# Loading each token-pair tile by four transfers of one head in place of one transfer of four heads

## The chip, the cores, the metric

One core of a Trainium2 chip. The metric is the device time of one launch in microseconds (us). Run-to-run spread is about 1 us for the kernel before. Times within a trace count from the start of its span, which is about 1.7 us shorter than the device time. "Granted clock" is the share of its full clock that TensorE was given; PSUM is the memory into which this kernel's matmuls write.

## The reference

```python
def _attn_ref(q, k, v):                       # q, k, v: (8, 8, 576, 64) float32
    scores = (1/sqrt(64)) * q @ k^T
    Dmat = where(rel >= 0, gamma[h] ** rel, 0)    # rel = query position - key position
    return (scores * Dmat) @ v

def reference(q, k, v, w_gate, w_val, w_out):
    x = attn_out.transpose(0, 2, 1, 3).reshape(4608, 512)
    return (sigmoid(x @ w_gate) * (x @ w_val)) @ w_out     # d_ff = 1536
```

## The kernel before

Everything is loaded by one instruction queue, SP (SyncE), in program order. First come the tokens of two "pairs" (a pair is 256 tokens, two neighbouring tokens on one partition), then the FFN weights, then a third pair between the rows of the output weights (wo), then the per-step loads of the rest.

```python
ld_pool = ctx.enter_context(tc.tile_pool(name="ld", bufs=18))
PAIRS = [(0, 0), (0, 1), (1, 0)]

def load_pair(A):
    b, a2 = PAIRS[A]
    for nm, src, g in (("k", k, 0), ("q", q, 0), ("k", k, 1), ("q", q, 1), ("v", v, 0), ("v", v, 1)):
        t = ld_pool.tile([P, M, 2, D], FP32, tag="ld", name=f"{nm}32p_{A}_{g}")   # M = 4 heads, 256 KB
        nc.sync.dma_start(out=..., in_=...)          # the change is here
        parts[nm, "pair", A, g] = t
        yield

for A in range(2):
    for _ in load_pair(A):
        pass
load_w(0, 2); load_w(2, 2); load_w(4, 4); load_w(8, 4)      # 24 tiles of 256 KB
pair_2 = load_pair(2)
for n_wo, n_pair in ((2, 4), (6, 2), (4, 0)):               # 2 wo, k q k q, 6 wo, v v, 4 wo
    ...
```

Each tile is cast as a whole, then transposed, multiplied and so on. This is what POOL and ACT do around the third pair:

```python
# ... cut: FFN of the first 512 tokens, whose matmuls run on TensorE between these lines
turn("k", 2, 0, tr_psum, "tr")     # turn: transpose on TensorE, copy out of PSUM on ACT
cast_wo(3, on_act)
turn("q", 2, 0, pv_psum, "pv")
cast_wo(4, on_pool)
turn("k", 2, 1, tr_psum, "tr")
turn("q", 2, 1, pv_psum, "pv")
# ... cut
cast_pair("v", 2, 1, on_pool)
cast_wo(9, on_pool); cast_wo(11, on_pool)      # wo 8 and 10 on ACT
loads_to(1)                                    # v, k, q of steps 0 and 1
# ... cut
later_constants()                              # mask tri, on POOL
for t in vbd[2:4]:
    nc.gpsimd.memset(t, 0.0)
casts_to(1)                                    # k, q of step 0 on POOL, then DMA transpose T, then v
```

T is a DMA transpose of step 0's k and q; the first per-step matmul (qk) needs it.

## Time and profile before

| | before |
|---|---|
| device time, median of 3 runs | 336.96 us |
| TensorE busy | 328.0 us of a span of 335.4 |
| first FFN matmul, hg | 19.60 us |
| first weight issued by SP / last wo tile landed | 9.90 us / 46.20 us |
| T landed / first qk that reads it | 57.11 us / 57.61 us |

The table of windows for the kernel before cuts the span at hg, at the landing of the last wo tile, and at the first qk. Its columns are the stretch and its length, then the busy time of each engine (with counts), TensorE's granted clock, the share of the DMA engines and GB/s:

```profile
0.00:19.60 19.60, 16.12 (x249) 8.49 (x249) 12.52 (x38) 11.90 (x24) 11.48 (x24) 1.00 0.99 275
19.60:46.20 26.60, 26.60 (x177) 12.55 (x178) 16.62 (x26) 14.20 (x26) 16.07 (x24) 1.00 1.08 349
46.20:57.60 11.40, 11.05 (x121) 6.06 (x119) 4.45 (x8) 4.85 (x11) 10.37 (x19) 1.00 0.74 149
57.60:335.40 277.80, 274.27 (x2242) 157.17 (x2240) 130.57 (x259) 136.84 (x285) 147.25 (x262) 1.00 0.81 157
```

TensorE is full from hg on, and the DMA engines are full until the last wo tile. The landing time of T is its issue at 53.33 us plus the 3.8 us that the tile view gives.

### The profile page before, as it was taken

What the parts mean: (1) busy time and instruction counts of PE and PEld (TensorE: products, weight loads), DVE (VectorE), ACT (ScalarE), POOL (GpSimd) and SP (SyncE); (2) the same over time, 40 slices, a digit from 0 to 9 for tenths busy, and PEclk for the clock granted to TensorE, in tenths of its full rate; (3) what the DMA queues carried; (4) which work ended last, traced back from release to release, by engine and by line L of the source; (5) the groups of instructions that cost most, each with busy time, mean ns of one, the idle gap of its engine ahead of it and who ended that gap; (6) DMA issues with size and microseconds to landing.
All of it is one profiled execution on the core that took longest, in us unless ns stands there. A gap on an engine that the chain in (4) does not pass through costs nothing.

```text
span 335.4 us, 7396 instructions
## 1 busy us (share of the span) xinstructions
PE 328.0 (98%) x2784; PEld 184.3 (55%) x2784; DVE 164.2 (49%) x328; ACT 167.8 (50%) x345; POOL 185.2 (55%) x327
## 2 busy tenths in 40 slices
PE   7999999999999999999999999999999999999996
PEld 3544445969666566556566555445555455444443
DVE  5744755726376356436346635542574156503320
ACT  6545635637565456355456655445646455233321
POOL 5655679779868798882448966582577500000000
PEclk9999999999999999999999999999999999999999
DMA  7999996799999999999976999499773850020002
GB/s 210 313 372 359 335 255 131 139 225 201 174 214 193 186 205 211 214 247 214 225 132 125 185 240 199 106 232 247 136 135 82 254 203 2 0 95 33 0 31 96
DMA packets 164100, 60.00 MB, mean 179 GB/s; under 512 B 144480, under 2 KB 156000, under 8 KB 164064
## 3 DMA queue, kind: packets, MB, share of 16 engines
q1 hardware_dynamic: 163920, 59.39, 83.2%
q8 instruction: 22, 0.36, 0.5%
q10 hardware_dynamic: 144, 0.13, 0.1%
q14 instruction: 14, 0.11, 0.1%
HBM read 37.75 MB, written 9.44 MB: 141 GB/s over the span
## 4 chain that ended last, share of the span: by engine, by line
PE 94%; DMA 2%; DVE 1%; SPq 1%; issue 1%; ACT 0%; POOL 0%
PE h L495 49%; PE op L561 24%; PE op L745 3%; PE hg L610 3%; PE hv L610 3%; PE pv L420 2%; PE qk L399 2%; PE pv L418 2%; DMA k32p<-in_k_dram 2%; PE st L432 2%; SPq L114 1%; PE op L551 1%; PE pvp L370 1%; PE idle L159 1%; PE st L345 0%
## 5 line engine op out<-in xcount | busy, mean ns | idle before, releaser
L495 PE MATMUL h<-xT,wg_sb 128*128 128x384 bf16 (+2 forms) x480 | 102.8, 337 | 0.2 <-DVE gv L523 0.2
L495 PE MATMUL h<-xT,wv_sb 128*128 128x384 bf16 (+2 forms) x480 | 102.8, 337 | 0.0
L252 POOL TENSOR_TENSOR qk_nat<-k,ktab 64x256 bf16<-64x256 f32 x120 | 73.3, 611 | 42.9 <-PE st L432 27.5
L523 DVE TENSOR_TENSOR gv<-g,h 128x384 bf16<-128x384 bf16 (+1 forms) x96 | 59.6, 621 | 71.8 <-PE h L495 56.4
L561 PE MATMUL op<-wo_sb,gv 128*128 128x512 bf16 x372 | 85.5, 379 | 0.0
L519 ACT ACTIVATE g<-h 128x384 bf16<-128x384 f32 (+1 forms) x96 | 52.2, 544 | 64.9 <-PE h L495 58.3
L438 DVE CAST sbd<-st 64x256 bf16<-64x256 f32 x104 | 43.7, 420 | 45.1 <-PE st L432 42.9
L495 PEld LDWEIGHTS <-wg_sb 128*128 128x128 bf16 x480 | 43.7, 98 | 31.4 <-issue 0.4
L495 PEld LDWEIGHTS <-wv_sb 128*128 128x128 bf16 x480 | 44.1, 98 | 29.0 <-issue 0.4
L273 POOL CAST vbd<-v 64x256 bf16<-64x256 f32 x120 | 47.4, 395 | 15.2 <-PE pv L420 10.6
L561 PEld LDWEIGHTS <-gv 128*128 128x128 bf16 x372 | 34.4, 98 | 36.3
L538 ACT COPY ob<-op 128x512 f32<-128x512 f32 x33 | 19.3, 585 | 47.5 <-PE op L561 42.8
L283 ACT CAST vs<-v 64x256 bf16<-64x256 f32 x104 | 41.9, 403 | 1.6
L262 POOL TENSOR_TENSOR qk_nat<-q,qtab 128x512 bf16<-128x512 f32 (+1 forms) x34 | 35.4, 1041 | 2.6
L422 ACT CAST xT<-pv 128x512 bf16<-128x512 f32 (+1 forms) x34 | 18.1, 534 | 18.1 <-PE pv L420 18.0
L401 DVE TENSOR_TENSOR pt<-qk,tri 128x512 bf16<-128x512 f32 (+1 forms) x34 | 21.2, 625 | 6.1 <-PE qk L399 5.8
L420 PE MATMUL pv<-pt,vbd 128*128 128x64 bf16 x240 | 18.0, 193 | 0.0
L432 PEld LDWEIGHTS <-qk_nat 128*128 128x128 bf16 x208 | 13.2, 98 | 8.8
L420 PEld LDWEIGHTS <-vbd 128*128 128x128 bf16 x240 | 15.2, 98 | 3.5
L418 PE MATMUL pv<-T,sbd 128*128 128x64 bf16 x216 | 17.2, 193 | 0.0
L511 DVE TENSOR_TENSOR gv<-g,h 128x256 bf16<-128x256 bf16 x24 | 10.0, 420 | 13.7 <-ACT g L509 13.3
L418 PEld LDWEIGHTS <-sbd 128*128 128x128 bf16 x216 | 15.1, 98 | 2.5
(76 smaller groups left out, 232.8 us busy)
## 6 DMA issues: line engine op xcount, KB each, us to landing
out_dram<-ob SPq DMA_DIRECT2D x34, 256.0 KB, 2.8
v<-in_v_dram SPq DMA_DIRECT2D x26, 256.0 KB, 4.1
k<-in_k_dram SPq DMA_DIRECT2D x26, 256.0 KB, 4.6
q<-in_q_dram SPq DMA_DIRECT2D x26, 256.0 KB, 5.1
wg<-in_moe_w_gate_dram SPq DMA_DIRECT2D x12, 256.0 KB, 6.0
wv<-in_moe_w_val_dram SPq DMA_DIRECT2D x12, 256.0 KB, 5.8
wo<-in_moe_w_out_dram SPq DMA_DIRECT2D x12, 256.0 KB, 5.4
k32p<-in_k_dram SPq DMA_DIRECT2D x6, 256.0 KB, 5.6
```

What stands on the lines that cost most here:

```text
L252: nc.gpsimd.tensor_tensor(out=kn[half(hh), j, :, half(hh)], in0=k32[half(j), hh::2, :], in1=ktab[half(j), c, hh::2].unsqueeze(2).to_broadc ...
L262: nc.gpsimd.tensor_tensor(out=qs[0:n], in0=q32[0:n], in1=qtab[0:n, c, :].unsqueeze(2).to_broadcast([n, H, D]), op=ALU.mult)
L273: nc.gpsimd.tensor_copy(out=vb[half(hh), j, :, half(hh)], in_=v32[half(j), hh::2, :])
L283: nc.scalar.copy(out=natural["vs", s][half(hh), j], in_=loaded[s][0][half(j), hh::2, :])
L401: nc.vector.tensor_tensor(out=pt[:, :, 0:n].rearrange("p m (j t) -> p m j t", t=64), in0=qkp[:, :, 0:n].rearrange("p m (j t) -> p m j t", ...
L418: nc.tensor.matmul(pvp[:, m, half(j)], lhsT=before[:, m, :], rhs=qT[:, m, half(j)], start=True, stop=False)
L420: nc.tensor.matmul(pvp[:, m, half(j)], lhsT=vb[:, j, m, :], rhs=pt[:, m, half(j)], start=before is None, stop=True)
L438: nc.vector.tensor_copy(out=sb[half(hh), :, half(hh)], in_=st_tiles[b][half(hh)])
L495: nc.tensor.matmul(out, lhsT=w_sb[:, kc, fc * P:(fc + 1) * P], rhs=xT[:, kc, t0 + a:t0 + e], start=(kc == 0), stop=(kc == NKC - 1))
L519: nc.scalar.activation(out=g[:, 0:n], in_=h1[:, 0:n], func=AF.Sigmoid)
L523: nc.vector.tensor_tensor(out=gvs[some[0]][:, a:e], in0=g[:, 0:n], in1=h2[:, 0:n], op=ALU.mult)
L561: nc.tensor.matmul(opp, lhsT=gvs[fc][:, nb * P:(nb + 1) * P], rhs=wo_sb[:, fc, :], start=(fc == 0), stop=(fc == NFC - 1))
```

## The change

Intent: an earlier start of the first tiles, as each head's piece can land by itself. Bytes and layout are the same.

```diff
             t = ld_pool.tile([P, M, 2, D], FP32, tag="ld", name=f"{nm}32p_{A}_{g}")
-            nc.sync.dma_start(
-                out=t.rearrange("p h r d -> p h (r d)"),
-                in_=src[b, g * M:(g + 1) * M, a2 * 2 * P:(a2 + 1) * 2 * P, :].rearrange("h (p r) d -> p h (r d)", r=2))
+            for h in range(M):
+                nc.sync.dma_start(
+                    out=t[:, h].rearrange("p r d -> p (r d)"),
+                    in_=src[b, g * M + h, a2 * 2 * P:(a2 + 1) * 2 * P, :].rearrange("(p r) d -> p (r d)", r=2))
```

## The prediction

> **What bounds the kernel now.** I read the page first. TensorE is busy 98% of the span and is 94% of the chain that ended last, so once TensorE is fed, the end lies a fixed amount of matmul work later. The question is therefore when TensorE gets fed. In forty slices (8.4 us each) its row shows the one soft place, the first slice, and the row of the DMA engines shows them full there:
>
> ```profile
> PE   7999999999999999999999999999999999999996
> DMA  7999996799999999999976999499773850020002
> ```
>
> Second, the chain of waits in order of time, restricted to the start. From 4.11 to 10.01 us the chain is a token pair load (the first k tile of the second pair), then a POOL cast, then a densely packed row of small matmuls up to the first FFN matmul (hg) at 19.60 us:
>
> ```profile
> 4.11 5.90 DMA k32p<-in_k_dram
> ...
> 10.08 1.05 POOL kp L242
> ...
> 14.54 1.29 DVE ptp L335 x2
> ...
> 19.60 1.02 PE hg L610 x4
> ```
>
> From hg on nearly every piece is TensorE work, so a later hg moves the end by the same amount. Third, the timeline of the SP queue, which issues every load (start, duration, what). It shows the pieces that the change multiplies, a kind with the shape of the new pieces (weight and output rows: one run per partition), and the issue of the first weights, which stands behind all twelve pair tiles:
>
> ```profile
> 1.32 0.49 SPq L114 DMA_DIRECT2D q32p<-in_q_dram  x1
> 1.85 0.51 SPq L114 DMA_DIRECT2D k32p<-in_k_dram  x1
> 2.40 0.51 SPq L114 DMA_DIRECT2D q32p<-in_q_dram  x1
> ...
> 9.90 1.34 SPq L126 DMA_DIRECT2D wg<-in_moe_w_gate_dram  x2
> ...
> 34.06 1.80 SPq L132 DMA_DIRECT2D wo<-in_moe_w_out_dram  x4
> ...
> 223.85 2.04 SPq L533 DMA_DIRECT2D out_dram<-ob  x4
> ```
>
> Fourth, the consumers. The casts on POOL begin as each tile lands; each has an idle time ended by the DMA:
>
> ```profile
> 3.94 1.04 POOL L242 TENSOR_TENSOR kp<-k32p,ktab 128x512 bf16<-128x512 f32 x1 [1.02 <-DMA k32p<-in_k_dram]
> 6.33 1.04 POOL L242 TENSOR_TENSOR kp<-k32p,ktab 128x512 bf16<-128x512 f32 x1 [1.35 <-DMA k32p<-in_k_dram]
> 10.08 1.04 POOL L242 TENSOR_TENSOR kp<-k32p,ktab 128x512 bf16<-128x512 f32 x1 [0.31 <-DMA k32p<-in_k_dram]
> 11.88 1.04 POOL L242 TENSOR_TENSOR kp<-k32p,ktab 128x512 bf16<-128x512 f32 x1 [0.76 <-DMA k32p<-in_k_dram]
> ```
>
> So in the first 15 us the kernel is bound by the pair loads: 256 KB land every 0.9 us (10.08 to 11.88 is two tiles), near 290 GB/s.
>
> **What the Trainium skill says.** "DMA: Bandwidth & Descriptors", section "Rules for kernel authors", says to coalesce small transfers, and that under 64 KB one pays mostly overhead; the new pieces are exactly 64 KB. "Issuing engines are not separate DMA queues", same page, calls the sequencer's time to start a DMA usually small relative to the DMA. The trace agrees for 256 KB (0.49 to 0.51 us of issue against 0.9 us of transfer); for 64 KB it cannot hold, since an estimated quarter of the transfer, 0.22 us, is less than half an issue. "Perfetto Trace Analysis", "What 'DMA-bound' means", names this state: the issuing sequencer's track is solid DMA slices.
>
> **The change part by part.** Bytes, and runs of 512 B, stay the same. Each pair tile takes 4 issues in place of 1: 18 issues become 72. The built order of SP confirms it (229 rows become 277, with repeats folded) and keeps the order of everything else. The first 12 tiles, 48 issues, still stand ahead of the first weight. The order also shows that the eight completion semaphores are used in rotation, so at most 8 pieces (512 KB) are in flight, where 8 tiles (2 MB) were; and each consumer now waits on four semaphores.
>
> Cost of one issue when they follow each other: the four wo issues took 1.80/4 = 0.45 us, the four stores 2.04/4 = 0.51; the pair issues 0.51 plus 0.04 of gap. The new pieces have one run per partition, like wo and stores, so I take 0.48 us from start to start (estimate). Eight of these are 3.8 us, more than a piece's landing time, so the rotation should not stop them. Landing time: the first 256 KB took 3.0 us (the tile view's minimum); less three quarters of 0.9, about 2.1 to 2.3; I take 2.1.
>
> Tile j (from 0) is then complete at 0.80 + 0.48(4j+3) + 2.1 = 4.3 + 1.92j. The last q tile of the second pair (j = 9), whose cast began at 12.74 before, lands at 21.6: 8.9 us later. The last v tile (j = 11) lands at 25.5, against 14.4. From the q tile on I walk the chain: cast 0.7, transpose and copy to 23.5, qk, the two masks on DVE at 1.29 us a pair (23.0 to 24.3, 24.75 to 26.05), v cast at 26.1, then st, filler matmuls, pv and the copy to xT, 2.3 us more: hg at about 28.4 in place of 19.6. **+8.8 us.** The small matmuls and fillers between wait inside that time and add nothing.
>
> Weights: first issue at 0.80 + 48 x 0.48 = 23.8 in place of 9.90. The first two wg tiles land about 26.7 and 27.5 and are cast by 28.2, just ahead of hg. At the 351 to 384 GB/s that the table of windows gives for 15 to 25 us, 256 KB come every 0.68 to 0.75 us, against 0.86 us of matmul per tile (3.45 us per 16). So the stream holds, with its former 4 us of lead gone: +0 to 1 us.
>
> The third pair, loaded between wo tiles at 29.3 to 38 us: 24 issues in place of 6. The DMA queue is full there, so the first eight pieces only wait for older tiles; the next eight run at 0.48 and leave the DMA engines half idle. My walk has its tiles land 10.1, 10.4, 11.5 and 12.6 us later than before while TensorE is 8.8 later: +1.4 us of stall at their transposes. The following v tiles come 13.4 later against a little slack: +0.7. The first per-step loads (v, k, q after wo) come about 14 us later against 2 us of slack at POOL's casts at 49.53; I give +1.5. Sum: 8.8 + 1.4 + 0.7 + 1.5 = 12.4, so 337 + 12 = **349 us**.
>
> **The rivals.** (1) The loads stay hidden: a quicker issue. A store issued after a pause needs only about 0.33 us, and at 0.37 start to start the same formula gives the q tile 4.3 us less delay: +4.5 at hg, and with half of the rest about 343. For it: smaller transfers generate fewer runs per issue. Against it: the two fours above, which are the back-to-back case. (2) The earlier first piece helps: consumers could start at the first head. The code casts a whole tile and the built order has the cast wait for all four semaphores, so no gain. (3) Eight semaphores in rotation become the wait: if a piece landed in 4.8 us, the pace would be 0.6 us and hg would slip by another 39 x 0.12 = 4.7 us: about 354. Against it: the first landing, 3.0 us for four times the bytes. (4) TensorE's clock: the skill's "TensorE: Matmul & The Clock Gate", "HAM oscillation", says idle gaps above about 3.4 us bring back half rate. The page before shows a granted clock of 9 tenths or more throughout; my walk leaves gaps of 1 to 2 us, so I expect little, at worst 2 us more.
>
> **Range and chances.** 343 is the quick-issue case, 355 the rotation case or the clock case, so **343 to 355** should hold it 8 times in 10. Slower by over 2% means over 343.7: 0.88. Within 2%: 0.11 (quick issue, or the later stalls absorbed). Faster: 0.01, as nothing on the path gets shorter.
>
> **What would show it.** SP's timeline: 48 pieces spaced by 0.45 to 0.5 us and the first wg issue at 23 to 25 us. The share of DMA in the first two slices falls while SP is solid. Fourth k cast near 20 us. First hg near 28.4. Later: a wait of about 1 us before the third pair's transposes, and hg to the end longer by 2 to 4 us than the 315.8 of before. It is wrong if pieces are spaced by 0.37 or less, if their landing takes over 4 us, or if the stages after hg give time back.

## The result

The changed kernel takes 357.34 us (median of 4 runs, 356.8 to 358.44) against 337.41 for the kernel before in the same rounds. The ratio is 1.0594, with a 95% interval of 1.0558 to 1.063. A ratio is the mean time of one kernel's runs over that of the other's of the same rounds, so it is not quite the ratio of the medians. The direction was right; the size was 20 us in place of 12, outside the predicted range. All outputs are right.

The page of the changed kernel, in forty slices of the span (8.9 us each): TensorE, its granted clock, and the DMA engines.

```profile
PE   6679976989999999999999999999999999999996
PEclk9859998999999999999999999999999999999999
DMA  4449958969999999999998599969964790011002
```

TensorE is now soft in six of the first nine slices, not in one. The DMA engines are half idle in the first three and in the sixth. The granted clock falls twice, right where TensorE is thin.

SP's queue in the changed kernel (start, duration, what, count):

```profile
2.67 1.85 SPq L115 DMA_DIRECT2D q32p<-in_q_dram  x4
4.57 1.85 SPq L115 DMA_DIRECT2D k32p<-in_k_dram  x4
...
15.97 3.14 SPq L115 DMA_DIRECT2D k32p<-in_k_dram  x4
...
24.85 0.95 SPq L127 DMA_DIRECT2D wg<-in_moe_w_gate_dram  x2
```

A tile of four pieces starts every 1.90 us, 0.475 us a piece, with no pause in between: SP's track is solid while the DMA engines are about half idle (a share of 0.54 up to hg). One tile is slower, 3.14 us. The weights are issued 15 us later than before.

The table of windows, cut at the same three events:

```profile
0.00:30.58 30.58, 20.28 (x246) 10.33 (x250) 12.24 (x37) 12.15 (x24) 10.44 (x22) 0.78 0.54 148
30.58:67.00 36.42, 30.31 (x217) 13.64 (x221) 17.73 (x26) 14.69 (x27) 17.13 (x26) 0.95 0.85 277
67.00:78.05 11.05, 9.14 (x82) 4.99 (x78) 5.30 (x10) 5.83 (x14) 10.01 (x19) 1.00 0.77 154
78.05:356.10 278.05, 272.85 (x2213) 157.16 (x2240) 129.39 (x255) 135.75 (x282) 148.09 (x262) 1.00 0.82 157
```

Up to hg the loss is 11.0 us. From hg to the last wo landing it is 36.42 - 26.60 = 9.8 us more. The last two rows are as long as before, within 0.4 us. So everything was lost before the last wo tile landed, at 67.00 us in place of 46.20.

TensorE's waits after hg, from its timeline (the bracket is the idle time before, and what ended it):

```profile
49.84 0.40 PE L312 MATMUL kTp<-ident,kp 128*128 128x128 bf16 x4 [1.20 <-POOL kp L243]
...
53.68 0.40 PE L312 MATMUL kTp<-ident,kp 128*128 128x128 bf16 x4 [1.50 <-POOL kp L243]
...
57.97 0.38 PE L312 MATMUL qTp<-ident,qp 128*128 128x128 bf16 x4 [3.03 <-ACT qT L322]
...
78.05 0.41 PE L400 MATMUL qk<-T 128*128 128x64 bf16 x8 [1.40 <-DMA T<-qk_nat]
```

It looks as if the third pair's transposes cost 5.7 us, and ACT the most of it. That reading fell in the experiments. The chain of waits of the changed kernel, followed back from the end, does not go through these transposes; before the first qk it goes through POOL, and before that through the load of a wo tile:

```profile
62.27 4.73 DMA wo<-in_moe_w_out_dram
67.00 0.05 issue
67.06 0.62 POOL wo_sb L225
...
73.08 1.04 POOL qk_nat L263
...
74.15 3.86 DMA T<-qk_nat
78.00 0.05 issue
78.05 0.41 PE qk L400 x8
```

The same place in the kernel before, POOL and TensorE from the timeline:

```profile
46.25 0.61 POOL L224 CAST wo_sb<-wo 128x512 bf16<-128x512 f32 x1 [0.83 <-DMA wo<-in_moe_w_out_dram]
52.26 1.04 POOL L262 TENSOR_TENSOR qk_nat<-q,qtab 128x512 bf16<-128x512 f32 x1
57.61 0.40 PE L399 MATMUL qk<-T 128*128 128x64 bf16 x8
```

POOL takes the same 7 us from the wo cast to T's issue in both kernels (46.25 to 53.33, 67.06 to 74.15). Before, T landed at 57.11 and TensorE came at 57.61 without a wait: it was the later one by half a microsecond.

### The profile page after: what moved, and what is told of

Read it like the earlier page. It is cut to its first block, busy times and chain, and to the rows that moved or that the text cites. A ratio compares the mean times of both kernels' runs of the same rounds, so it can differ in the third digit from the quotient of the medians. Undisturbed runs are those within 1.5% of the kernel's fastest.

```text
span 356.1 us, 7450 instructions
## 1 busy us (share of the span) xinstructions
PE 332.6 (93%) x2749; PEld 186.1 (52%) x2784; DVE 164.7 (46%) x328; ACT 168.4 (47%) x345; POOL 185.7 (52%) x327
## 3 DMA queue, kind: packets, MB, share of 16 engines
q1 hardware_dynamic: 164784, 59.40, 79.4%
## 4 chain that ended last, share of the span: by engine, by line
PE 76%; SPq 9%; DMA 8%; issue 3%; POOL 2%; DVE 1%; ACT 1%; DVEq 0%
PE h L496 45%; PE op L562 22%; SPq L115 7%; DMA wo<-in_moe_w_out_dram 4%; DMA wg<-in_moe_w_gate_dram 3%; PE pv L421 2%; PE qk L400 2%; PE pv L419 2%; PE st L433 2%; SPq L127 1%; DMA T<-qk_nat 1%; PE op L552 1%; POOL qk_nat L253 1%; DVE ptp L336 0%; PE hv L611 0%
## 5 line engine op out<-in xcount | busy, mean ns | idle before, releaser
L562 PE MATMUL op<-wo_sb,gv 128*128 128x512 bf16 x356 | 84.5, 379 | 0.8
L433 PEld LDWEIGHTS <-qk_nat 128*128 128x128 bf16 x208 | 13.2, 98 | 8.8
L419 PE MATMUL pv<-T,sbd 128*128 128x64 bf16 x216 | 17.2, 193 | 0.0
```

Of the source, the lines that this page charges most:

```text
L419: nc.tensor.matmul(pvp[:, m, half(j)], lhsT=before[:, m, :], rhs=qT[:, m, half(j)], start=True, stop=False)
L562: nc.tensor.matmul(opp, lhsT=gvs[fc][:, nb * P:(nb + 1) * P], rhs=wo_sb[:, fc, :], start=(fc == 0), stop=(fc == NFC - 1))
```

## The experiments

Twelve kernels ran. First the table that they give together; each time is from the profiled run of that kernel, and the ratio from all its timed runs. "whole" means unsplit pair tiles.

| kernel | hg | last wo landed | T landed | first qk | span | ratio to before |
|---|---|---|---|---|---|---|
| before | 19.60 | 46.20 | 57.11 | 57.61 | 335.4 | 1 |
| the change | 30.58 | 67.00 | 78.00 | 78.05 | 356.1 | 1.0594 |
| first_two | 30.09 | 59.40 | 70.39 | 70.43 | 347.9 | 1.0376 |
| third | 19.74 | 54.08 | 65.02 | 65.45 | 343.1 | 1.0191 |
| two_halves | 22.51 | 49.97 | 60.87 | 60.91 | 338.6 | 1.0098 |
| empty_issues (whole) | 31.30 | 59.73 | 70.68 | 71.32 | 348.8 | 1.0398 |
| empty_all (whole) | 29.98 | 67.29 | 78.25 | 78.30 | 356.0 | 1.0604 |
| split_wo_late | 32.25 | 66.03 | 76.98 | 77.03 | 355.0 | 1.0589 |
| third_wo_late | 20.27 | 52.47 | 63.38 | 63.43 | 341.1 | 1.0190 |
| whole_wo_late | 20.19 | 46.69 | 57.69 | 58.20 | 336.0 | 1.0003 |
| split_warm | 29.14 | 65.54 | 76.51 | 76.56 | 355.6 | 1.0557 |
| split_T_early | 29.73 | 65.56 | 75.17 | 76.05 | 354.1 | 1.0540 |
| split_both | 30.00 | 65.61 | 74.82 | 74.87 | 352.9 | 1.0519 |
| whole_T_early | 19.60 | 45.81 | 55.09 | 57.62 | 335.4 | 0.9991 |

From the first qk to the end is 277.5 to 278.1 us in every row but split_warm, which has 279.1. The kernels of first_two, split_wo_late, split_T_early and split_both are the changed kernel up to hg, and still hg lies between 29.73 and 32.25 us in these five rows: a difference of 1 or 2 us at hg between two single profiles shows nothing. T lands 10.9 to 11.0 us after the last wo tile in every row but the three in which POOL's order was changed.

### Which loads cost: first_two and third

```diff
-            for h in range(M):                     # four pieces, all pairs
+            if A < 2:                              # first_two;   third: if A == 2
+                for h in range(M): ...             # four pieces
+            else:
+                nc.sync.dma_start(...)             # one transfer
```

> Only the two pairs loaded ahead of the weights are split, the third pair stays whole. Theory (issue time at the start sets hg, the third pair has a cost of its own): hg at 30.6 us as in the changed kernel (30.58), then half or more of the later loss gone: 348.5 to 351. Rival (the later loss is only the lost lead of the weights, not the third pair's own pieces): 355 to 357. Rival (the start costs what I predicted and the rest is the third pair): 346 to 347.

Measured: 349.92 us (349.46 to 350.58), +3.8%; hg at 30.09.

> Only the third pair is split. Theory: hg at 19.6 us as before, then TensorE waits at the third pair's transposes, above all the last q one, whose copy on ACT stands behind the cast of a wo tile that is now issued after 16 pieces: 341 to 344. Rival (the 4 us of lead that the weights still have here hides it): 337 to 339.

Measured: 344.28 us (341.69 to 344.78), +1.9%, a little above the range that I gave; hg at 19.74.

The two parts add up: 3.8% and 1.9% make 5.7% of the 5.9%. In terms of the last wo landing they are +13.2 and +7.9 us, together 21.1 of the measured 20.8. So the third pair's 18 extra issues cost 7.9 us, close to their issue time (18 x 0.475 = 8.6), though the weights had their lead there. But issue time is not the only wait there. SP's waits between 41 and 64 us in the changed kernel, for the pieces of the third pair (total us, times, longest):

```profile
SPq L115 <- DMA wo<-in_moe_w_out_dram: 2.5, 5, 1.1
SPq L115 <- DMA wv<-in_moe_w_val_dram: 1.3, 4, 0.3
SPq L115 <- DMA wg<-in_moe_w_gate_dram: 0.6, 2, 0.3
```

Each of these eleven issues waits for a semaphore that an older tile holds (the one at 59.03 us for the wo tile that landed at 59.01), as eight completion semaphores are used in rotation. SP stood 4.4 us for them in all. At the start no piece waits so. No run gives the third pair more semaphores, so how its 7.9 us divide between issue time and this limit of eight transfers in flight is not shown.

### Half the split: two_halves

```diff
+            for h in range(0, M, 2):
+                nc.sync.dma_start(out=t[:, h:h + 2]..., in_=src[b, g * M + h:g * M + h + 2, ...]...)
```

> Every pair tile in two transfers of two heads. Theory (the issue rate of SP against the landing rate): two issues at about 0.52 us are 1.04 us a tile, little over the 0.9 us at which whole tiles landed, so hg slips by only 0.5 to 1.5 us and the first wg issue moves from 9.9 to about 13.3: 338 to 340. Rival (cost goes by the size of a transfer or by the number of semaphores waited for, so half the split costs about a third to a half): 344 to 348.

Measured: 340.74 us (339.62 to 341.41), +1.0%, between the theory's range and the rival's, and far nearer the theory's. SP needs 0.51 us from start to start (4.37, 4.89, 5.40 us), so 1.03 us a tile against the 0.9 us at which whole tiles landed. hg came 2.9 us late, more than the 0.5 to 1.5 that I expected. A slow stretch is part of it: the transfer issued at 9.49 us landed 2.0 us after the one before it. Cost is not in proportion to the number of pieces. The three points (0.55 us of issue a tile before, 1.03 and 1.90) fit a cost that sets in where the issue time of a tile passes its transfer time.

### Issues alone, tiles whole: empty_issues and empty_all

```diff
             nc.sync.dma_start(out=t..., in_=...)                # whole tile, as before
+            for x in range(3 if A < 2 else 0):                  # empty_all: range(3)
+                nc.sync.dma_start(out=spare[:, at:at + 4], in_=k[0, x, 0:P, 0:4])
+                at += 4
```

> Kernel before with whole tiles, but each of the first twelve pair tiles is followed by three transfers of 16 bytes a partition into a spare tile that nobody reads: the 36 issues of the split without the split. Right results. Theory (SP's issue time): period about 1.95 us a tile, first wg issue near 24 us, hg near 28 to 30.5 us, 347 to 351, as in the run that splits the first two pairs alone. Rival (64 KB transfers, pieces in flight or four semaphores a cast are the cost): 337 to 340.

Measured: 350.82 us (350.0 to 351.38), +4.0%; hg at 31.30, first weight issued at 25.24 us.

> Kernel before with whole tiles, and three empty issues of 16 bytes a partition after every one of the 18 pair tiles, the third pair too. Right results. Theory (the whole loss is issue time in SP's queue, which delays the last wo tile; the end follows that landing, and the two stretches add): last wo tile lands at 66 to 67.5 us, as in the changed kernel (67.00), 355.5 to 358.5. Rival (the third pair's cost is its small pieces or their semaphores): 350 to 352, as with 36 empty issues.

Measured: 357.62 us (357.29 to 359.1), +6.0%; last wo tile landed at 67.29 us (67.00 in the changed kernel). SP's queue in empty_all:

```profile
4.79 0.44 SPq L117 DMA_DIRECT2D k32p<-in_k_dram  x1
5.27 1.45 SPq L121 DMA_DIRECT2D spare<-in_k_dram  x3
6.77 0.43 SPq L117 DMA_DIRECT2D q32p<-in_q_dram  x1
7.25 1.45 SPq L121 DMA_DIRECT2D spare<-in_k_dram  x3
```

An issue of 2 KB that nobody reads takes the same 0.48 us as one of 64 KB. These kernels have the whole tiles of before, one semaphore per cast for each tile, and the whole loss. This settles what costs: neither the split of the tiles nor the number of semaphores that a cast waits for is needed for it. The extra issues are enough. At the start they cost by SP's time alone; in the third pair the empty issues wait in the rotation of eight as the pieces do, so the two stay together there.

### Is it ACT's order? split_wo_late, third_wo_late, whole_wo_late

My second theory was built on the 3.03 us above. ACT stood in front of wo tile 3, which is issued after 16 pieces of the third pair, so ACT could not empty the PSUM buffer that TensorE's last q transpose needed.

```diff
-    cast_wo(3, on_act)
     turn("q", 2, 0, pv_psum, "pv")
 ...
     turn("q", 2, 1, pv_psum, "pv")
+    cast_wo(3, on_act)
```

> The changed kernel, with one ACT instruction moved: the cast of the wo tile number 3 stands after the copy of the third pair's last transpose in place of before the q copy of its first half. Theory (ACT stands in front of a late wo tile and keeps a PSUM buffer that TensorE's last q transpose needs): that transpose comes at about 55.7 us in place of 57.97, the end 2 to 4 us earlier than the changed kernel: 353.5 to 355.5. Rival (the last q tile's own landing at 54.7 us is the whole wait): 356.5 to 358.

Measured: 357.19 us (356.76 to 357.78), +5.9%: no change.

> The same move in the kernel that splits the third pair alone, where TensorE stood 4.66 us for ACT's copy. Theory: 2.1 us of the wait stay (the q tile's landing), 2.5 go, and with the shorter pause the granted clock does not fall to a half: 340 to 342 in place of 344.3. Rival: 343.5 to 345.

Measured: 343.98 us (342.77 to 344.28), +1.9%: no change (third had 1.9% too).

> Control: the same move in the kernel before. Theory (wo tile 3 lands there just in time, so ACT's order costs nothing): 336.5 to 338, same as before. Rival (the move is a gain by itself, whatever the loads): 334 to 336.

Measured: 337.45 us, ratio 1.0003 (0.9988 to 1.0018): no change, as expected.

The theory is half right, and of no use for the time. TensorE's timeline in split_wo_late:

```profile
55.28 0.40 PE L312 MATMUL qTp<-ident,qp 128*128 128x128 bf16 x4 [0.18 <-DVE qp L243]
...
77.03 0.41 PE L400 MATMUL qk<-T 128*128 128x64 bf16 x8 [1.98 <-DMA T<-qk_nat]
```

The wait at the transpose is gone (0.18 in place of 3.03 us), and the wait for T has grown (1.98 in place of 1.40). In third_wo_late the wait, which had been 4.66 us in third, fell to 0.52 the same way. What was taken from TensorE's chain was given back at T, since T hangs on the load stream. In third itself T had landed only 0.4 us before TensorE came (65.02 and 65.45), so no more than that was to be gained.

### Is it the clock? split_warm

```diff
     turn("k", 0, 0)
+    fill(4)                        # filler matmuls, no result
     turn("q", 0, 0)
-    fill(4)
+    fill(9)
 ... cut: seven more places, 35 more fillers in all (the expectation says 37)
```

> The changed kernel with 37 more filler matmuls in front of the transposes at which TensorE stood idle in the first 25 us; the loads are untouched. Theory (about 1 to 1.5 us of the loss up to hg is the granted clock, which fell to 0.5 to 0.77 between 10 and 30 us): clock 1.0 through the start, hg near 29.5 in place of 30.58, 355 to 356.5. Rival (landing times alone set hg, the clock costs nothing there): clock 1.0 and 357 to 358.

Measured: 356.65 us (355.17 to 357.33), ratio 1.0557 (1.0532 to 1.0583), whose interval overlaps that of the changed kernel: not settled. What the profile settles is the clock. In the table of windows for 10 to 30 us, the changed kernel has a mean granted clock of 0.66 and split_warm 1.00:

```profile
10.00:30.00 20.00, 14.49 (x219) 7.98 (x222) 7.74 (x12) 6.90 (x14) 5.77 (x8) 0.66 0.58 161
```

```profile
10.00:30.00 20.00, 16.19 (x244) 8.49 (x238) 8.05 (x13) 7.28 (x15) 5.15 (x7) 1.00 0.57 159
```

hg came at 29.14 us, earlier than in the five profiles that are alike up to there (29.73 to 32.25), but by an amount that one profile can't tell. TensorE then waited 1.80 us for the second weight tile in the middle of hg: the loads were behind it all the same. After that wait the clock fell again (0.66 from 30 to 35 us), so this run does not show the kernel at full clock throughout.

### Is it T? split_T_early, split_both, whole_T_early

The third theory: two chains meet at the first qk, and in the changed kernel the chain of the loads is the later one. The last wo landing, POOL's work behind it and T make it. POOL's order can be changed without touching a load before the last wo tile.

```diff
     cast_pair("v", 2, 1, on_pool)
+    later_constants()
+    for t in vbd[2:4]:
+        nc.gpsimd.memset(t, 0.0)
     cast_wo(8, on_act)
 ... and both taken out of their place behind the cast of wo 11
-        for nm, src in (("v", v), ("k", k), ("q", q)):
+        for nm, src in ((("k", k), ("q", q), ("v", v)) if s == 0 else (("v", v), ("k", k), ("q", q))):
```

> The changed kernel with the load stream up to the last wo tile untouched; on POOL the mask and memset work that stood between the cast of the last wo tile and the first per-step k cast is moved ahead of it, and step 0 loads k, q, v in place of v, k, q. Theory (the end follows the first DMA transpose T, which follows the last wo landing through POOL): T is issued 1.5 to 2.5 us sooner after that landing, TensorE's wait of 1.4 us at its first per-step qk goes: 1.0 to 1.8 us below the changed kernel, 355.5 to 356.5. Rival (TensorE's own earlier stalls set the end): no change, 357 to 357.8.

Measured: 355.73 us (355.33 to 356.17), ratio 1.0540 (1.0522 to 1.0558).

> The same two moves and the moved ACT cast, which alone gave nothing. Theory (two chains, TensorE's and the load stream's, end at the first per-step qk; ACT's move shortened only the first, which was not the later one): now both are shorter, about 2 us below the changed kernel: 354.8 to 355.8. Rival: the ACT move is worth nothing here either, so as split_T_early alone, 355.5 to 356.5, or 357 and more if neither matters.

Measured: 354.63 us (354.26 to 356.47), ratio 1.0519 (1.0495 to 1.0543). This one has the moved ACT cast too.

> Control: the moves on POOL and the load order of step 0 in the kernel before. There T landed 0.5 us before TensorE came to it, so TensorE's chain is the later one. Theory: 336.7 to 337.6, no gain. Rival (the moves are a gain by themselves): 335 to 336.

Measured: 337.11 us, ratio 0.9991 (0.9976 to 1.0005): no gain.

TensorE at the first qk, in split_T_early, then in whole_T_early:

```profile
76.05 0.40 PE L400 MATMUL qk<-T 128*128 128x64 bf16 x8
```

```profile
57.62 0.40 PE L399 MATMUL qk<-T 128*128 128x64 bf16 x8
```

In both TensorE no longer waits for T. In split_T_early T landed at 75.17, 0.9 us ahead (9.6 us after the last wo tile in place of 11.0; that tile itself came 1.4 us earlier in this profile), so TensorE's chain had become the later one; that is where the ACT move could count, and with both the first qk came at 74.87. By their medians the T moves took 1.6 us off the changed kernel and the ACT move, worth nothing alone, perhaps 1.1 more; the intervals of these two kernels overlap, so the second step is likely and not shown. In the kernel before, T came 2 us earlier and the time stayed, because TensorE was already the later chain there.

No experiment beats the kernel before. The best form of the split into four is still 5.2% behind it, and the two controls are equal to it.

## Why the prediction was wrong

**Right by its own steps.** The pieces follow each other at 0.475 us (0.48 predicted), and land after a median of 2.1 to 2.3 us (2.1). The first weight is issued at 24.85 (23.8; "23 to 25"). The fourth k cast starts at 20.92 ("near 20"). The casts wait for whole tiles, so no early piece helps. The eight semaphores in rotation never stopped the pieces at the start: the gap between two issues stays 0.04 us. They did later, in the third pair. The first two rivals are refuted, the quick issue (0.37 us) and the early piece. One reading was wrong without harm: that the trace agrees with "usually small" at 256 KB. There 0.55 us from start to start against 0.9 us of transfer is three fifths, so the queue had little to spare.

**Off in size, hg.** Predicted 28.4, measured 30.58. Of the 2.2 us, about 1.1 are a slow tile: the 3.14 us line at 15.97 in place of 1.85, after which the last q tile landed at 22.68 in place of 21.6. About 1 is the slower chain behind it: cast of that tile to hg took 7.8 us (22.80 to 30.58), 6.9 before. In that stretch the granted clock was 0.5 to 0.7. The fourth rival was named and put at "little, at worst 2 us"; it happened, without the long gaps that I thought it needed, and what it cost is not shown. These parts are of one profile.

**The step that failed** is the last term of the sum: "The first per-step loads (v, k, q after wo) come about 14 us later against 2 us of slack at POOL's casts at 49.53; I give +1.5." They came 20.9 us later (v of step 0 landed at 68.18 in place of 47.28), as the last wo tile did (+20.8). Two errors are in it. They account for the whole gap: my delay of 14 us less 2 of slack is 12, and 20.8 less 0.5 is 20.3; the first qk came 20.4 us later.

The first is size, 6.8 us of it. Pair loads of the third pair came 13.4 us late at their first tile where I had 10.1. A part is the slow tile. The rest is the weights: in my walk they won back about 1 us (the first landed 11.3 us late, the tile behind the last 10.1), and in the trace they lost 1 (27.74 us in place of 15.38 for the first, 46.10 in place of 32.65 for the last). From there to the last wo tile I let the first eight pieces pass for free and got about 4 us. The trace shows 7.4 (13.4 to 20.8), and the run that splits the third pair alone shows 7.9. The first eight pieces did pass almost free (13.6 us late at the second tile). The next eight brought the delay to 17.2 us where I had 12.6, the six wo tiles behind them to 18.8, and the last four wo tiles from 18.9 to 20.8. In front of these four the queue held eight pieces, which landed 0.2 us apart (60.62 to 62.28 us), faster than SP issued.

The second, 1.5 us, is the path. I walked TensorE's chain, added up its stalls and read the slack of the load stream at POOL's k cast at 49.53 (v of step 0 had landed at 47.28, k at 48.41). But the path runs through POOL's cast of the last wo tile at 46.25, and there POOL had stood waiting for the load (0.83 us), so it had no slack. The stream is a chain of its own: last wo tile, POOL for 7 us, T, first qk. It had 0.5 us of slack before, at T. A chain with 0.5 us of slack that is delayed by 20.8 us delays the end by about 20.3, whatever TensorE does meanwhile: the first qk moved by 20.4 and the span by 20.7. The third pair's stalls, ACT's order and the clock all lie inside this delay. That is why taking the ACT wait away changed nothing, and moving T did.

What the runs leave open is how much the clock alone is worth in the time (split_warm's median is 0.7 us below that of the changed kernel, within the noise), and how the third pair's cost divides between issue time and the eight semaphores.

## What to carry to other kernels

Count issues before bytes: where transfers follow each other on one queue, compare start-to-start issue time with the transfer time of each, and split only while the first is the smaller. For the price of a delay in a load queue, do not add up the waits of the busiest engine; follow the last load of the stage through its consumers to the place where it meets that engine, and look up how much slack it had there. A wait that is removed and comes back elsewhere tells that another chain was the later one.

## What the Trainium skill lacked or had wrong

- "DMA: Bandwidth & Descriptors", "Rules for kernel authors", has transfers under 64 KB as mostly overhead. Here the split to 64 KB made the kernel 5.9% slower and the split to 128 KB still 1.0% slower: for a queue that is nearly issue-bound at 256 KB (0.51 us of issue plus 0.04 against 0.9 of transfer), the 64 KB of that row are no safe limit.
- The same page, "Issuing engines are not separate DMA queues", calls the issue time usually small relative to the DMA. Here it is 0.55 us against 0.9 us of transfer at 256 KB, and 0.475 us against 0.22 us at 64 KB (four pieces landed 0.22 us apart from 47.69 to 48.35 us); the extra issues brought the whole loss. No section of it lists start-to-start times by shape on this queue; these runs show 0.475 us for one run per partition, 0.51 for two, 0.55 for four, and the same 0.475 whether the piece has 2 KB or 64 KB.
- "TensorE: Matmul & The Clock Gate", "HAM oscillation", warns of idle gaps above about 3.4 us. Here the granted clock fell to 0.50 between 20 and 25 us although the longest gap between matmuls in the first 30 us after the opening fillers was 1.40 us; TensorE had been busy 2.08 of 5 us between 5 and 10 us. With fillers in the gaps it stayed at 1.00 from 10 to 30 us, although the longest gap that ended there was 1.42 us. So the length of a gap alone told nothing here. The page's next section, "A second HAM failure mode: psum-queue depth-cycling", does name short pauses as a cause in another kernel.
- No page names packets of 16 KB on a queue of the kind "instruction" as a disturbance of loads; "Runtime: NRT & Kernel Launch", "Instruction fetch mechanics", describes refills in blocks of that size and calls their cost mostly hidden. Each trace has 22 such packets, of 0.9 to 1.9 us each. One starts at 15.76 us in the changed kernel, and SP's slow issue (1.71 us) follows at 15.97 us; another starts at 49.14, with a slow issue (1.34 us) at 49.28. In each of the fourteen traces an SP issue of 0.9 to 1.8 us starts within 0.8 us of the first of these packets, in the kernel before too (12.51 and 12.82 us), where the loads kept landing. The packets come after similar counts of TensorE's weight loads from the fourth on (485, 617 and 735 in the changed kernel; 483, 612 and 734 before), so they look like that engine's instruction fetch; this is inferred, and no run tested it.
